# Retention and SwiGLU block on one core: keys and values of pairs five to eight loaded once, by token, one head per half of the partitions

## The chip, the cores and the metric

The kernel runs on one NeuronCore of a Trainium2 chip. The core has five engines, each with an instruction stream of its own that it works through in order: TensorE (PE in the profile, its weight loads PEld), VectorE (DVE), ScalarE (ACT), GpSimd (POOL) and SyncE (SP, which only issues transfers). ACT and POOL can issue transfers too. The metric is device time in microseconds; the time before is the median of three runs, 1016.25 us (1015.04 to 1018.67).

## The reference

Batch 8, 8 heads, 576 tokens, 64 dimensions per head, all float32; then a feed-forward block with 512 model dimensions and 1536 hidden ones on 4608 tokens.

```python
scores = scale * np.matmul(q, k.transpose(0, 1, 3, 2))
gamma = 1.0 - 2.0 ** (-5.0 - np.arange(H))
Dmat = np.where(rel >= 0, gamma[:, None, None] ** rel[None, :, :], 0.0)   # rel = query position - key position
ret = scores * Dmat[None, :, :, :]
attn_out = np.matmul(ret, v)
x = attn_out.transpose(0, 2, 1, 3).reshape(B * S, H * D)
g = x @ w_gate
silu = g * (1.0 / (1.0 + np.exp(-g)))
return silu * (x @ w_val) @ w_out
```

## The kernel before

**Attention.** A *pair* i is two heads of one batch: batch i // 4, heads 2p and 2p + 1 with p = i % 4; there are 32 pairs. A head's 576 tokens are 9 *chunks* of 64. Inside a chunk the scores are computed and masked; what earlier chunks contribute goes through a running 64x64 *state* per head (keys times values, scaled by a power of gamma). Every matmul of the attention is 64x64, in a quarter of the TensorE array: rows by the half of the partitions in which the operands lie, columns by the half in which the result comes out.

**One tick.** `tick(t)` moves three pairs on by one stage. On TensorE, in this order: `own_values(t-2)` (masked scores times values, inside chunks), `new_states(t-1)` (keys times values into `z`), `earlier_values(t-2)` (state times query), `scores(t-1)` (into `sc`). Then come *pieces* for the other engines, for ticks 4 to 9 in this order: `copies` of pair t-1 (L584: ScalarE copies half of `z` out of PSUM into `even`) and `keys` of pair t (L507: ScalarE scales the keys in place); `outputs` of pair t-2 (L629, L658: VectorE scales results into `x_odd`); the mask `own` of pair t-1 (L580: VectorE multiplies `sc` by the decay table `near` into `ret`); `last`, `pairs`, `odd`, `evens` (L590, L596, L603, L608: VectorE builds the states); and two VectorE transposes by 32x32 blocks (L492) that make `qT` and `kT` of pair t. `sc` and `z` share the two PSUM banks of the tile `inner`: columns 0 to 255 of each bank hold scores, columns 256 to 511 hold `z`. `kT` is one buffer: it can be rewritten only after `scores(t-1)` has read it.

**Loads.** For pairs 4 and up `load(i)` brings q and k in an arrangement of 32x32 blocks (L282, four transfers each) that the block transpose turns into a full transpose, and, for the "whole" pairs 4 to 19, k a second time and v once by token (L287, one transfer each, the two heads' tokens running through all 128 partitions). `chunk(i, hl, c)` says in which half of the partitions and in which columns chunk c of head hl lies: in whole pairs the half alternates with the chunk. So in `own_values` the even and the odd chunks of a whole pair are two groups, and an empty instruction on TensorE that waits for the first group stands ahead of `earlier_values` (L549).

**The weights and the first token tile.** While pairs 4 to 9 go through, TensorE computes the first 512 tokens of the feed-forward block: `up0(f)` for f = 0 to 11 (L853) writes the gate product of hidden block f into bankA and the value product into bankB for even f, bankC and bankE for odd f; ScalarE then reads the first (Silu, L856) and VectorE the second (L857). `down0` (L864) follows and uses the four banks in the order A, B, C, E. The weights come as 18 blocks of 1 MB in raw form; each half block j goes through `split(j)` (two ScalarE instructions, L389 and L390) and `rounding(j)` (two VectorE instructions, L406 and L407), two buffers deep: `split(j + 2)` overwrites what `rounding(j)` has read. The next raw block is requested from ScalarE's queue (from SP's for the first five) after a split. Blocks 24 and 28 (j) hold the weights of f = 10.

**The order.** Everything is issued in the order in which it is written (`manual_schedule`), and each engine keeps it. The list `plan` weaves the parts: tick 4 after the first rounding, ticks 5, 6, 7, 8, 9 after `up0` of f = 3, 5, 7, 10, 11. GpSimd has `end_loads` (L687, L692: 20 transfers for the last chunk of the first batch) ahead of all this, and its sums of output weights (L886) behind. Lines 701 to 726 (`end_...`) deal with that last chunk of the first batch in ticks 6 and 7.

Of the kernel before, what the change touches and what calls it, by code (L numbers as in the profile page):

```python
# [22 lines left out]
def tables(gamma, scale, L):  # L23

    g, at = np.array(gamma), np.arange(L)
    lane = np.arange(2 * L)[:, None]
    both = lambda t: np.repeat(t, L, axis=0).reshape(-1, 2 * L, t.shape[1]).transpose(1, 0, 2).reshape(2 * L, -1)
    twice = lambda t: np.concatenate([t, t])
    half = [np.repeat(g.reshape(-1, 2), L, axis=1).T ** (lane % 32 + 32 * r) for r in range(2)]
    pieces = scale * np.stack(half, axis=2).reshape(2 * L, -1)
    runs = scale * (g[None, :, None] ** ((4 * lane[:, :, None] + np.arange(4)) % L)).reshape(2 * L, -1)
    parts = [twice((g[:, None] ** -at).T), twice((g[:, None] ** (L - at)).T),
             both(g[:, None] ** L), both(g[:, None] ** (2 * L)), pieces, runs, both(scale * g[:, None] ** at),
             both((scale * g[:, None] ** at).reshape(-1, 2, L)[:, ::-1].reshape(-1, L))]  # L40
    return np.concatenate(parts, axis=1).astype(np.float32)


# [88 lines left out]
def kernel(  # L132
# [107 lines left out]

    loaded = {}

    def whole(i):

        return HP <= i < needed(2) - 2

    def scaled(i):

# [5 lines left out]
    def load(i):  # L254

        b, p = divmod(i, HP)
        t = kp.tile([P, NC * D], F32, tag="v", name="v", bufs=4)
        late = [rest[:, dn_at + 1280 * (i - 2) + 640 * n :][:, 0 : NC * D] for n in range(2)] if 1 < i < HP else None
        kn = late[1] if late else kp.tile([P, NC * D], F32, tag="kn", name="kn")
        queue = nc.sync  # L260
        if i < HP:
            qk = late[0] if late else ld.tile([P, 2, S // SQ, SQ], F32, tag="qk", name="qk").rearrange("p n j d -> p (n j d)")[:, 0 : NC * D]
            queues = (nc.sync, nc.scalar if i < 2 else nc.sync)
            heads = range(2 * p, 2 * p + 2)
            blocks = lambda a: a[:, 0:CW].rearrange("p (c h d) -> p h c d", h=2, d=D)
            for h, queue in zip(heads, queues):
                if scaled(i):
                    queue.dma_start(out=early[i][:, ts(h % 2, CW // 2)], in_=q[b, h, 0:CW].rearrange("(p c) d -> p (c d)", c=NFULL))
                else:
                    queue.dma_start(out=blocks(qk)[:, h % 2], in_=q[b, h, 0:CW].rearrange("(c p) d -> p c d", p=P))  # L270
            for h, queue in zip(heads, queues):
                queue.dma_start(out=blocks(kn)[:, h % 2], in_=k[b, h, 0:CW].rearrange("(c p) d -> p c d", p=P))
            for h in heads:
                queues[i % 2].dma_start(out=blocks(t)[:, h % 2], in_=v[b, h, 0:CW].rearrange("(c p) d -> p c d", p=P))
        else:
            if i == needed(1) - 3:
                qk = rest[:, 4096 : 4096 + 2 * S].rearrange("p (n j d) -> p n j d", n=2, d=SQ)
            else:
                qk = ld.tile([P, 2, S // SQ, SQ], F32, tag="qk", name="qk")
            for n, src in enumerate((q, k)):  # L280
                for a in range(P // SQ):
                    queue.dma_start(  # L282
                        out=qk[a * SQ : (a + 1) * SQ, n],
                        in_=src[b, 2 * p + a // 2, :, (a % 2) * SQ : (a % 2 + 1) * SQ].rearrange("(j t) d -> t j d", t=SQ))
            for dst, src in ((kn, k), (t, v)):
                if whole(i):
                    queue.dma_start(out=dst.rearrange("p (g d) -> p g d", d=D), in_=tokens(src, b, p))  # L287
                    continue
                for hl in range(2):
                    queue.dma_start(out=dst[:, 0:CW].rearrange("p (c h d) -> p c h d", h=2, d=D)[:, :, hl, :],  # L290
                                    in_=src[b, 2 * p + hl, 0:CW, :].rearrange("(c p) d -> p c d", p=P))
            if not whole(i):
                queue.dma_start(out=t[:, CW : CW + D], in_=v[b, 2 * p : 2 * p + 2, CW:S, :])
        loaded[i] = (qk, kn, t)

    def chunk(i, hl, c):

        if whole(i):
            g, r = divmod(NC * hl + c, 2)
            return half[r], slice(g * D, (g + 1) * D)  # L300
        if c + 1 == NC:
            return half[hl], slice(CW, CW + D)
        return half[c % 2], slice((2 * (c // 2) + hl) * D, (2 * (c // 2) + hl + 1) * D)
# [144 lines left out]
    def transposes(i):  # L448
# [34 lines left out]
        else:  # L483
            if light(i):
# [3 lines left out]
                    for r in range(2):  # L488
                        nc.scalar.activation(out=src[:, r], in_=src[:, r], func=AF.Copy, scale=piece[:, 2 * p + r : 2 * p + r + 1])
                pieces.append(scale_q)  # L490
            for n, t in enumerate((qT, kT)):
                pieces.append(lambda n=n, t=t: nc.vector.transpose(out=t, in_=qk[:, n].rearrange("p j d -> p (j d)")))  # L492

        every = slice(0, P)

        def keys():
            blocks = kn.rearrange("p (g d) -> p g d", d=D)
# [12 lines left out]
            return [lambda: (keys(), pieces[0]())] + pieces[1:]  # L510
        return [keys] + pieces

    straight, exchanged = [(slice(0, P), slice(0, P))], [(half[0], half[1]), (half[1], half[0])]

    def value(i, hl, c):

# [7 lines left out]
    def own_values(i, n=0):  # L524

        s, ret = st[i], places(i)[0]
        cs = [a + d for a in (1 - n, 5 - n) for d in (0, 2)] if whole(i) else range(0 if n else NC - 1)
        for c in cs:
            for hl in range(2):
                rows, at = chunk(i, hl, c)  # L530
                start = n == 0 and c in (cs[:2] if whole(i) else (0, 1))
                m = nc.tensor.matmul(value(i, hl, c), s["v"][rows, at], ret[rows, c % 2 if whole(i) else hl, c // 2],  # L532
                                     start=start, stop=start, skip_group_check=True)
        if n == 0:
            s["own"] = m
# [26 lines left out]
    def scores(i, alone):  # L562
# [6 lines left out]
        for c in range(NFULL):  # L569
            for hl in range(2):  # L570
                for r in range(2):
                    at = ts(2 * c + r, L)
                    nc.tensor.matmul(sc[chunk(i, hl, 2 * c + r)[0], r if whole(i) else hl, c], kT[half[hl], at], qT[half[hl], at],
                                     start=True, stop=True, skip_group_check=True)

    def masked(i):
        p, (ret, ret_last, state) = i % HP, places(i)

        def own():
            nc.vector.tensor_tensor(out=ret, in0=sc, in1=near[:, 2 * p : 2 * p + 2].unsqueeze(2).to_broadcast([P, 2, NFULL, L]),  # L580
                                    op=ALU.mult)

        def copies():
            (nc.vector.tensor_copy if vector(i + 1) else nc.scalar.copy)(out=even, in_=z[:, 0])  # L584

        odd_states = state[:, 1:].rearrange("p (c r) d -> p c r d", r=2)[:, :, 1]
# [96 lines left out]
    def end_loads():  # L683
# [5 lines left out]
                        in_=src[0, a // 2 : H : 2, CW + j * SQ : CW + (j + 1) * SQ, (a % 2) * SQ : (a % 2 + 1) * SQ].rearrange("n t d -> t n d"))  # L689
        for hl in range(2):  # L690
            for x in range(2):
                nc.gpsimd.dma_start(out=end_v[half[hl ^ x], 2 * x : 2 * x + 2],  # L692
                                  in_=v[0, 4 * x + hl : 4 * x + 4 : 2, CW:S].rearrange("n t d -> t n d"))

    def end_transposes():
# [9 lines left out]

    def end_masks():
        for x in range(2):
            nc.vector.tensor_tensor(out=end_ret[:, 2 * x : 2 * x + 2], in0=end_at[x], in1=near[:, 5 * x : 5 * x + 3 : 2], op=ALU.mult)

    def end_own(x):  # L710
        for n, _, hl in [e for e in ends if e[1] == x]:
            rows = half[hl ^ x]
# [24 lines left out]
    def tick(t, lo=HP, hi=NP, spread=False, then=None):  # L737
# [832 lines left out]
```

## Time and profile before

| | |
|---|---|
| median of three runs | 1016.25 us (1015.04, 1016.25, 1018.67) |
| the profiled execution | 1014.55 us, of which 1012.8 us is the span from its first to its last instruction |
| granted TensorE clock | 1.000 |
| busy in the span | PE 99%, PEld 82%, DVE 70%, ACT 28%, POOL 55% |
| mean DMA rate | 192 GB/s |
| mean busy share of the 16 DMA engines, first eight of 40 slices, tenths | 9 9 9 9 8 6 6 9 |
| transfer packets | 278892, of which 212552 are under 512 bytes |

Times in the timeline count from the start of the span. The busy shares are averages over very different stages: tick 4's transposes run at 43 us, ticks 5 to 9 begin on TensorE at 54.8, 70.0, 86.5, 110.3 and 119.6 us. In rows of instructions the first number is the start, the second the duration; what stands in brackets is the time that the engine was idle before it and what ended the wait. A group of several instructions in one row ("x3") has the time from its first start to its last end.

### The profile page before, as it was taken

How to read it: one execution, taken by the hardware profiler on the slowest of the kernel's cores; microseconds unless marked ns; L12 is line 12 of the kernel's file. 1: busy time of each engine (PE TensorE's matmuls, PEld its weight loads, DVE VectorE, ACT ScalarE, POOL GpSimd, SP SyncE). 2: the span in 40 equal slices, each digit the busy share in tenths (PEclk: the TensorE clock that was granted, in tenths of full speed). 3: DMA queues.
4: the chain of work that ended last, by engine and by line, in shares of the span. 5: the costliest groups of instructions: out<-in, count | busy, mean ns of one | idle time of the engine just before them, and what ended most of it. 6: DMA issues, size and time to landing. Idle time of an engine off the chain costs nothing.

```text
span 1012.8 us, 21319 instructions
## 1 busy us (share of the span) xinstructions
PE 1000.9 (99%) x8336; PEld 825.5 (82%) x8336; DVE 710.9 (70%) x1206; ACT 286.7 (28%) x636; POOL 561.8 (55%) x589
## 2 busy tenths in 40 slices
PE   6999999999999999999999999999999999999998
PEld 5655555888888888888888888888888888888887
DVE  4488887677875766977777678866575767566645
ACT  4565522132423312133422202233220012232110
POOL 3400359979375228575564157746672586566514
PEclk9999999999999999999999999999999999999999
DMA  9999866967587787647677777434454554445553
GB/s 245 261 288 272 192 216 234 264 193 214 138 238 207 217 231 193 198 156 196 184 202 206 198 179 217 154 133 159 161 172 141 154 189 147 148 155 180 182 159 102
DMA packets 278892, 194.38 MB, mean 192 GB/s; under 512 B 212552, under 2 KB 246088, under 8 KB 278792
## 3 DMA queue, kind: packets, MB, share of 16 engines
q1 hardware_dynamic: 251464, 94.70, 36.7%
q10 hardware_dynamic: 26688, 97.92, 29.1%
q8 instruction: 66, 1.08, 0.5%
q0 software_dynamic: 640, 0.39, 0.2%
q14 instruction: 34, 0.28, 0.1%
HBM read 154.04 MB, written 38.93 MB: 191 GB/s over the span
## 4 chain that ended last, share of the span: by engine, by line
PE 94%; DVE 2%; DMA 1%; POOL 1%; SPq 0%; issue 0%; ACT 0%; DVEq 0%; ACTq 0%; POOLq 0%
PE bankB L1186 12%; PE bankC L1186 11%; PE bankA L1186 11%; PE bankE L1186 11%; PE bankB L1392 7%; PE bankC L1392 7%; PE bankE L1392 6%; PE bankA L1392 6%; PE outer L532 2%; PE bankE L853 2%; PE bankA L853 2%; PE outer L1186 2%; PE inner L1186 2%; PE bankB L853 2%; PE outer L559 2%; PE bankC L853 2%
## 5 line engine op out<-in xcount | busy, mean ns | idle before, releaser
L1042 POOL TENSOR_TENSOR rest<-rest 128x512 f32<-128x512 f32 (+1 forms) x139 | 148.0, 1076 | 159.9 <-DVE rest L1042 112.5
L1201 POOL TENSOR_TENSOR arena<-rest,io 128x256 f32<-128x256 f32 x168 | 123.9, 750 | 89.4 <-ACT io L1200 88.9
L1200 ACT ACTIVATE io<-rest 128x256 f32<-128x256 f32 x192 | 79.3, 417 | 200.0 <-DVE rest L1042 140.0
L1186 PE MATMUL bankB<-rest,arena 128*128 128x256 f32 x448 | 114.5, 380 | 0.0
L1042 DVE TENSOR_TENSOR rest<-bankB,rest 128x512 f32<-128x512 f32 x116 | 78.5, 685 | 40.5 <-PE bankB L1186 28.5
L1186 PE MATMUL bankC<-rest,arena 128*128 128x256 f32 x416 | 106.3, 380 | 0.0
L1186 PE MATMUL bankA<-rest,arena 128*128 128x256 f32 x412 | 104.8, 379 | 0.0
L1042 DVE TENSOR_TENSOR rest<-bankA,rest 128x512 f32<-128x512 f32 x111 | 75.2, 685 | 40.8 <-PE bankA L1186 19.3
L1042 DVE TENSOR_TENSOR rest<-bankC,rest 128x512 f32<-128x512 f32 x110 | 74.5, 683 | 38.0 <-PE bankC L1186 23.4
L1042 DVE TENSOR_TENSOR rest<-bankE,rest 128x512 f32<-128x512 f32 x106 | 71.7, 684 | 36.2 <-PE bankE L1186 17.6
L1186 PE MATMUL bankE<-rest,arena 128*128 128x256 f32 x372 | 94.9, 380 | 0.3 <-DVE rest L1042 0.3
L1186 PEld LDWEIGHTS bankB<-rest,arena 128*128 128x128 f32 x448 | 84.7, 190 | 11.9 <-DVE rest L1042 0.2
L1186 PEld LDWEIGHTS bankC<-rest,arena 128*128 128x128 f32 x416 | 78.5, 190 | 11.4 <-DVE rest L1042 0.8
L1186 PEld LDWEIGHTS bankA<-rest,arena 128*128 128x128 f32 x412 | 78.1, 190 | 10.9 <-DVE rest L1042 0.2
L1186 PEld LDWEIGHTS bankE<-rest,arena 128*128 128x128 f32 x372 | 70.3, 190 | 10.4 <-DVE rest L1042 0.8
L1042 POOL TENSOR_TENSOR arena<-arena 128x256 f32<-128x256 f32 (+1 forms) x76 | 70.3, 947 | 11.1 <-PE bankC L1186 9.0
L886 POOL TENSOR_TENSOR rest<-rest 128x512 f32<-128x512 f32 x21 | 28.5, 1377 | 72.1 <-DVE rest L407 58.5
L1392 PE MATMUL bankB<-arena 128*128 128x256 f32 x264 | 61.0, 381 | 0.0
L1392 PE MATMUL bankE<-arena 128*128 128x256 f32 x264 | 60.8, 380 | 0.0
L1392 PEld LDWEIGHTS bankE<-arena 128*128 128x128 f32 x264 | 50.0, 190 | 6.9
L1392 PEld LDWEIGHTS bankB<-arena 128*128 128x128 f32 x264 | 49.8, 190 | 6.9
L1392 PE MATMUL bankC<-arena 128*128 128x256 f32 x240 | 55.2, 379 | 0.0
(270 smaller groups left out, 1876.0 us busy)
## 6 DMA issues: line engine op xcount, KB each, us to landing
arena<-up ACTq DMA_DIRECT2D x63, 896.0 KB, 4.6
arena<-dn ACTq DMA_DIRECT2D x65, 384.0 KB, 3.1
arena<-dn SPq DMA_DIRECT2D x39, 384.0 KB, 3.1
out_dram<-rest SPq DMA_DIRECT2D x31, 256.0 KB, 3.4
qk<-in_q_dram SPq DMA_DIRECT2D x108, 72.0 KB, 3.1
qk<-in_k_dram SPq DMA_DIRECT2D x108, 72.0 KB, 3.4
dn<-rest SPq DMA_DIRECT2D x26, 256.0 KB, 2.8
up<-arena SPq DMA_DIRECT2D x13, 512.0 KB, 5.6
```

The source lines that it names most:

```text
L532: m = nc.tensor.matmul(value(i, hl, c), s["v"][rows, at], ret[rows, c % 2 if whole(i) else hl, c // 2], start=start, stop=start, skip_grou ...
L559: nc.tensor.matmul(xr[half[hl]] if c + 1 == NC else value(i, hl, c), state[half[hl], c, :], s["qT"][half[hl], ts(c, L)], start=False, stop ...
L853: nc.tensor.matmul(bank, w, xs[0][:, c, :], start=(c == 0), stop=(c == HP - 1))
L886: eng.tensor_tensor(out=dst, in0=srcs[0], in1=srcs[1], op=ALU.add if op[0] == "add" else ALU.subtract)
L1042: eng.tensor_tensor(out=out, in0=a, in1=b, op=ALU.add if sign > 0 else ALU.subtract)
L1186: m = nc.tensor.matmul(b[:, g * TB : (g + 1) * TB], w[:, g], x, start=(opens and g == 0), stop=True, skip_group_check=True)
L1200: nc.scalar.activation(out=s, in_=src[:, 0:TB], func=AF.Silu)
L1201: (nc.vector if busy and o != 2 and qd + 1 < NQ else nc.gpsimd).tensor_tensor(out=hid[:, qd, 2 * H + h, 2 * T + t], in0=src[:, TB : 2 * TB ...
L1392: nc.tensor.matmul(b[:, m * TB : (m + 1) * TB], lhs[:, qd, ts(m, P)], w[:, qd], start=(opens and qd == 0 and m == 0), stop=(qd == NQ - 1), ...
```

## The change

Pairs 4 to 7 (the second batch) become "natural" pairs, and no longer count as whole. Their k and v are each loaded once, by token, with a head in each half of the partitions (two transfers each); the four transfers of k in blocks are gone. `turn_keys` makes `kT`: VectorE transposes `kn` by 32x32 blocks in one instruction, which leaves the two off-diagonal blocks of each 64x64 chunk in each other's place; GpSimd copies one of them aside (into the unused k half of the `qk` tile), and four ScalarE copies exchange them across the halves of 32 partitions. One ScalarE instruction then scales the keys with a new table column per pair (`own_key`) in place of two. `turn_keys` is issued first of a tick's pieces (ticks 4 to 7), where the transpose of k stood last and `keys` stood beside `copies`.

Since both operands of a head now lie in its own half, the results of odd chunks change halves: `new_states` writes odd chunks of `z` in the other half, ScalarE's copy brings them back in two instructions instead of one, and the mask `own` (ticks 5 to 8) becomes three VectorE instructions, one for even chunks and two that change halves for odd ones. The waiting instruction ahead of `earlier_values` is dropped for these pairs. The end pieces of the first batch are treated in the same way (`end_masks` three instructions instead of two).

```diff
+             np.repeat(g.reshape(-1, 2), L, axis=1).T ** (L - lane % L)]
...
+    def natural(i):
+        return HP <= i < 2 * HP
     def whole(i):
-        return HP <= i < needed(2) - 2
+        return 2 * HP <= i < needed(2) - 2
...
-            for n, src in enumerate((q, k)):
+            for n, src in enumerate((q,) if natural(i) else (q, k)):
...
+                if natural(i):
+                    for hl in range(2):
+                        queue.dma_start(out=dst[half[hl]].rearrange("p (c d) -> p c d", d=D),
+                                        in_=src[b, 2 * p + hl].rearrange("(c t) d -> t c d", t=L))
+                    continue
...
     def chunk(i, hl, c):
+        if natural(i):
+            return half[hl], slice(c * D, (c + 1) * D)
...
+    own_key = tab[:, NCOL + 2 * HP * L :]
...
-            for n, t in enumerate((qT, kT)):
+            for n, t in enumerate((qT,) if natural(i) else (qT, kT)):
...
+        def turn_keys():
+            kept = qk[:, 1, 0:NC]
+            at = kT.rearrange("p (c x t) -> p c x t", x=2, t=SQ)
+            nc.vector.transpose(out=kT, in_=kn)
+            nc.gpsimd.tensor_copy(out=kept, in_=at[:, :, 1])
+            for lo in (0, D):
+                one, two = slice(lo, lo + SQ), slice(lo + SQ, lo + D)
+                nc.scalar.copy(out=at[one, :, 1], in_=at[two, :, 0])
+                nc.scalar.copy(out=at[two, :, 0], in_=kept[one])
+            nc.scalar.activation(out=kn[:, 0:CW], in_=kn[:, 0:CW], func=AF.Copy, scale=own_key[:, p : p + 1])
+        if natural(i):
+            return [turn_keys] + pieces
...
-                    nc.tensor.matmul(z[half[hl], r, c], s["kn"][chunk(i, hl, 2 * c + r)], s["v"][rows, at],
+                    nc.tensor.matmul(z[half[hl ^ r if natural(i) else hl], r, c], s["kn"][chunk(i, hl, 2 * c + r)], s["v"][rows, at],
...
-        wait = nc.tensor.nop()
-        tc.add_manual_dep(wait.ins, s["own"].ins.name,
-                          mybir.DependencyInfo(mybir.DependencyClass.Sync, mybir.DependencyReason.DATA), reason="row halves")
+        if not natural(i):
+            wait = nc.tensor.nop()
+            tc.add_manual_dep(wait.ins, s["own"].ins.name,
+                              mybir.DependencyInfo(mybir.DependencyClass.Sync, mybir.DependencyReason.DATA), reason="row halves")
...
         def own():
+            if natural(i):
+                for rows, to, x in [(every, every, 0)] + [(*e, 1) for e in exchanged]:
+                    nc.vector.tensor_tensor(out=ret[to, x], in0=sc[rows, x], in1=near[rows, 2 * p + x].unsqueeze(1).to_broadcast(list(sc[rows, x].shape)),
+                                            op=ALU.mult)
+                return
...
         def copies():
+            if natural(i):
+                for rows, to in exchanged:
+                    nc.scalar.copy(out=even[to], in_=z[rows, 1])
+                return
...
-                    nc.vector.scalar_tensor_tensor(out=at, in0=even[:, c], scalar=step[:, p : p + 1], in1=z[:, 1, c],
+                    one, two = (z[:, 0, c], even[:, c]) if natural(i) else (even[:, c], z[:, 1, c])
+                    nc.vector.scalar_tensor_tensor(out=at, in0=one, scalar=step[:, p : p + 1], in1=two,
...
     def end_masks():
         for x in range(2):
-            nc.vector.tensor_tensor(out=end_ret[:, 2 * x : 2 * x + 2], in0=end_at[x], in1=near[:, 5 * x : 5 * x + 3 : 2], op=ALU.mult)
+            for rows, to in exchanged if x else straight:
+                nc.vector.tensor_tensor(out=end_ret[to, 2 * x : 2 * x + 2], in0=end_at[x][rows], in1=near[rows, 5 * x : 5 * x + 3 : 2], op=ALU.mult)
...
         outputs = to_x(t - 2)[0] if lo <= t - 2 < hi else lambda: None
+        if lo <= t < hi and natural(t):
+            pieces.append(keys)
+            keys = lambda: None
```

More of the change, by code (lines that the diff above doesn't have):

```diff
@@ L39, in tables @@
              both(g[:, None] ** L), both(g[:, None] ** (2 * L)), pieces, runs, both(scale * g[:, None] ** at),
-             both((scale * g[:, None] ** at).reshape(-1, 2, L)[:, ::-1].reshape(-1, L))]
+             both((scale * g[:, None] ** at).reshape(-1, 2, L)[:, ::-1].reshape(-1, L)),
+             np.repeat(g.reshape(-1, 2), L, axis=1).T ** (L - lane % L)]
     return np.concatenate(parts, axis=1).astype(np.float32)
@@ L291, in load @@
                                     in_=src[b, 2 * p + hl, 0:CW, :].rearrange("(c p) d -> p c d", p=P))
-            if not whole(i):
+            if not whole(i) and not natural(i):
                 queue.dma_start(out=t[:, CW : CW + D], in_=v[b, 2 * p : 2 * p + 2, CW:S, :])
@@ L511, in transposes @@
         return [keys] + pieces
-    straight, exchanged = [(slice(0, P), slice(0, P))], [(half[0], half[1]), (half[1], half[0])]
+    every = slice(0, P)
+    straight, exchanged = [(every, every)], [(half[0], half[1]), (half[1], half[0])]
     def value(i, hl, c):
@@ L527, in own_values @@
         cs = [a + d for a in (1 - n, 5 - n) for d in (0, 2)] if whole(i) else range(0 if n else NC - 1)
+        parity = whole(i) or natural(i)
         for c in cs:
@@ L531, in own_values @@
                 start = n == 0 and c in (cs[:2] if whole(i) else (0, 1))
-                m = nc.tensor.matmul(value(i, hl, c), s["v"][rows, at], ret[rows, c % 2 if whole(i) else hl, c // 2],
+                m = nc.tensor.matmul(value(i, hl, c), s["v"][rows, at], ret[rows, c % 2 if parity else hl, c // 2],
                                      start=start, stop=start, skip_group_check=True)
@@ L572, in scores @@
                     at = ts(2 * c + r, L)
-                    nc.tensor.matmul(sc[chunk(i, hl, 2 * c + r)[0], r if whole(i) else hl, c], kT[half[hl], at], qT[half[hl], at],
+                    rows = half[hl ^ r] if natural(i) else chunk(i, hl, 2 * c + r)[0]
+                    nc.tensor.matmul(sc[rows, r if whole(i) or natural(i) else hl, c], kT[half[hl], at], qT[half[hl], at],
                                      start=True, stop=True, skip_group_check=True)
@@ L691, in end_loads @@
             for x in range(2):
-                nc.gpsimd.dma_start(out=end_v[half[hl ^ x], 2 * x : 2 * x + 2],
+                nc.gpsimd.dma_start(out=end_v[half[hl], 2 * x : 2 * x + 2],
                                   in_=v[0, 4 * x + hl : 4 * x + 4 : 2, CW:S].rearrange("n t d -> t n d"))
@@ L707, in end_masks @@
         for x in range(2):
-            nc.vector.tensor_tensor(out=end_ret[:, 2 * x : 2 * x + 2], in0=end_at[x], in1=near[:, 5 * x : 5 * x + 3 : 2], op=ALU.mult)
+            for rows, to in exchanged if x else straight:
+                nc.vector.tensor_tensor(out=end_ret[to, 2 * x : 2 * x + 2], in0=end_at[x][rows], in1=near[rows, 5 * x : 5 * x + 3 : 2], op=ALU.mult)
     def end_own(x):
         for n, _, hl in [e for e in ends if e[1] == x]:
-            rows = half[hl ^ x]
+            rows = half[hl]
             m = nc.tensor.matmul(end_at[x][half[hl ^ x], n], end_v[rows, 2 * x + n], end_ret[rows, 2 * x + n],
```

## The prediction

> **What bounds the kernel now.** I read the busy time in stretches first: the start, the next 25 us, the tail, and the stretches in which the changed pairs run.
>
> ```profile
> 0.00:25.00 25.00, 17.36 (x406) 14.29 (x407) 12.54 (x29) 10.42 (x21) 9.14 (x17) 1.00 1.06 244
> 25.00:50.00 25.00, 24.82 (x197) 15.70 (x196) 11.81 (x24) 12.60 (x26) 12.51 (x23) 1.00 1.09 265
> 900.00:1012.00 112.00, 109.39 (x507) 95.95 (x505) 63.26 (x83) 20.13 (x42) 53.96 (x45) 1.00 0.49 156
> ...
> 55.00:73.00 18.00, 18.00 (x254) 9.69 (x251) 14.84 (x32) 11.68 (x22) 0.00 (x0) 1.00 1.09 298
> 90.00:113.00 23.00, 23.00 (x185) 11.19 (x184) 19.41 (x41) 14.74 (x27) 1.38 (x1) 1.00 1.04 265
> ```
>
> The columns after the length are PE, PEld, DVE, ACT and POOL, then clock, DMA share, GB/s. PE is busy 1000.9 of 1012.8 us. Of the 11.9 us left, 7.64 lie in the first 25 us, 0.18 in the next, 2.6 in the tail: some 1.5 us of waiting remain in all the rest. The start comes before the first changed transfer (28 us) and the tail is far behind the changed pairs, so waits that the change removes can give at most about 1.5 us. TensorE bounds the stage; VectorE follows at 82 to 84% there, and the transfers are saturated (share over 1) without holding TensorE up.
>
> So the question is how far VectorE and ScalarE may fall behind before TensorE feels it. The timeline around tick 7 and behind tick 8 answers:
>
> ```profile
> 89.58 0.37 ACT L584 COPY even<-inner 128x256 f32<-128x256 f32 x1 [2.38 <-PE inner L573]
> 90.52 0.69 DVE L580 TENSOR_TENSOR ret<-inner,near 128x512 f32<-128x512 f32 x1
> 95.48 0.43 DVE L406 TENSOR_SCALAR arena<-rest 128x512 int32<-128x512 int32 x1
> 95.94 0.68 ACT L389 ACTIVATE rest<-rest 128x512 f32<-128x512 f32 x1 [3.99 <-DVE arena L406]
> 100.19 0.60 ACT L856 ACTIVATE io<-bankA 128x512 f32<-128x512 f32 x1
> ...
> 103.27 1.45 PE L853 MATMUL bankA<-rest,arena 128*128 128x512 f32 x3
> ...
> 123.66 0.68 DVE L857 TENSOR_TENSOR arena<-bankE,io 128x512 f32<-128x512 f32 x1
> 124.38 0.30 PEld L864 LDWEIGHTS bankE<-rest,arena 128*128 128x128 f32 x2 [0.57 <-DVE arena L857]
> ```
>
> Read it backwards. After a tick's pieces VectorE goes on with a rounding (95.48), a ScalarE split waits for that (95.94), and splits and roundings hand over to each other until ScalarE reads bankA (100.19 to 100.79), the product of f = 8. TensorE wants bankA for f = 10 at 103.27. **First margin: 2.4 us.** Behind tick 8, VectorE's last read of bankE ends at 124.34, and the weight load of TensorE's next use of bankE had waited for it, 0.57 us against 0.24 between its neighbours. **Second margin: about 0.1 us.** VectorE's way there from tick 8's pieces (112.14) has no gap.
>
> **The change, part by part.** *Prices.* Exchange copies (32x288, four per tick): the trace has no such copy. A ScalarE scaling from SBUF to SBUF with 288 columns has 523 ns, with a number from a table; without one, 512 columns have 621 ns, and PSUM copies grow by 107 ns from 128 to 256 columns, so 288 columns are 0.43 us. Back to back such instructions overlap by about 0.1: 0.33 each; upper bound 0.43 each, from the 523 ns.
>
> ```profile
> L489 ACT ACTIVATE qk<-qk,tab 128x288 f32<-128x288 f32 x22 | 10.4, 523 | 0.0
> L917 ACT ACTIVATE rest<-rest 128x512 f32<-128x512 f32 x1 | 0.6, 621 | 0.0
> L626 ACT COPY rest<-outer 64x256 f32<-64x256 f32 x8 | 2.9, 367 | 0.1
> L1440 POOL COPY last_near<-near 128x256 f32<-128x256 f32 x1 | 0.4, 397 | 0.1
> ...
> DVE ret L580 <- ACT even L584: 13.6, 10, 2.3
> ```
>
> GpSimd's copy aside: 0.397 for 256 columns, so 0.45 for 288; upper bound 0.84, from its two-operand instruction (750 ns for 256). Key scaling: 549 ns for 320 columns grown to 512: 0.71, followed after 0.62. Copies of z: two at 0.37, the second ending 0.64 after the first starts. Masks: three 0.43 apart (as L629 x3, 1.28) against 0.6: +0.7 us of VectorE per tick. End masks +0.25.
>
> *The new chain.* The transposition of k stays one VectorE instruction (0.73) but moves ahead of the masks; behind it hang GpSimd's copy (0.04 + 0.45 + 0.04, hand-overs as between L584's end and L580's start at 29 us), four exchanges (1.32), the scaling (0.62), and only then, on ScalarE's queue, the copies of z (0.64 + 0.04): **3.15 us** from the end of the transposition. The last row above says what waits for them: VectorE's mask waits for ScalarE's copy of z ten times. Queued behind the copies on ScalarE are the next split, its weight request and the Silu; behind the mask on VectorE the states, the transpose of q and the roundings. The trace cannot tell whether each mask half waits for both copies; I let it. [...]
>
> *Tick 4* has no masks. GpSimd's queue is busy with `end_loads` until 46.5 us, so the copy aside ends at 46.95 and the rest on ScalarE at about 49, where ScalarE now waits for weights until 49.29: hidden. Those weights stand behind load(4) on SP, which loses 4.93 us of issuing (32.07 to 37.0), so they come earlier, and if GpSimd is free by 45, ScalarE is up to 1.7 us ahead (no more helps: tick 5's transposition needs `scores(4)`, over at 56.1). I take 1.0 ahead, range 0.3 to 1.7.
>
> *Tick 5.* VectorE reaches its pieces at 57.87 - 1.0 = 56.87; transposed 57.60; half masks from 60.75; `last`, two steps of 0.43 later, at 61.6 against 58.46: +3.15. The transposition (0.66) no longer comes at the end: the next rounding is 2.5 late. *Tick 6*: VectorE comes free at 71.86 + 2.5 (the read of bankE at 71.25 and 0.61 to the next instruction; its wait for TensorE until 72.61 absorbs the rest), `last` at 74.36 + 0.73 + 3.15 + 0.86 = 79.1 against 74.66: +4.4; outputs (1.45) run inside the wait. Next rounding -0.66 + 0.25: 4.0 late. *Tick 7*: free at 87.85 + 4.0 (likewise from the read at 87.24), `last` at 96.6 against 91.13: +5.45, next rounding 4.8 late.
>
> *First stall.* ScalarE's read of bankA ends at 100.79 + 4.8: 2.4 us too late for 103.27. *Second.* VectorE ends the roundings ahead of tick 8 at 109.96 + 4.8, the next read of bankB at 115.4, where TensorE (2.4 late) would have had it at 114.5: 0.9 behind, plus 0.7 of masks, less the margin of 0.1: 1.5 us. *On TensorE*: as many matmuls; the quarters now alternate without repeats and the waiting instruction is gone; 32 records take 0.47 us, and with at most a tenth of that to win per group it is -0.1 (0 to -0.3). *SP*: eight transfers instead of ten per pair; all come earlier. The wider table adds 16 bytes per partition: nothing. Later weight requests move with the splits that need them.
>
> Sum: 2.4 + 1.5 - 0.1 = **+3.8**; the span becomes 1016.6. The profiled execution had 1014.55 in all, 1.7 below the median; against the median 1016.25 the forecast is 1020.0.
>
> **Rivals.** *Absorbed* (+0.5 to +2.0, 1017.5): ScalarE gets its full 1.7 ahead at tick 4 (-0.7), halves wait singly (-0.8), the exchanges are shorter; the first stall nearly goes, the second, fed by masks, stays. For: 3.99 us of ScalarE idling at 95.94 shows that it has room. Against: its copies stand in one queue.
>
> *Not slower* (1015.5): the transfers decide. Four times 295 KB less, all in 128-byte pieces, in saturated stretches; weights arrive up to 4.9 us sooner, ScalarE works ahead of VectorE and both stalls vanish, up to 0.7 us of TensorE's remaining waits too. It decides if splits start before 45 us and tick 5 is not held by `scores(4)`. Against: only one ScalarE wait for weights over 1 us stands in the stage, at 49.29, and TensorE waits for none. [...]
>
> *Worse* (+5.2 to +7, 1022.3): the chain has the upper prices, 0.4 more on GpSimd and 0.4 on ScalarE per tick, 2.4 in three ticks, with VectorE slowed beside GpSimd (its L407 at 105.4 took 1.55 beside a GpSimd sum, else 0.69).
>
> **How the numbers follow.** Forecast (+2 to +5.2) 0.58, of which three quarters lie above +3.05, that is 0.3%, about what a measurement of this kernel can tell from no change; worse 0.17; absorbed 0.17; not slower 0.08, with 0.03 of it below -0.3% by the runs' own scatter (1015.0 to 1018.7). Slower 0.43 + 0.17 = 0.60; faster 0.03; same 0.37. Range 1016.6 (+0.4) to 1023.0 (+6.8).
>
> **What would show it.** In the changed profile: masks (L580's successor) starting over 3 us after the transposition of `kn` and right after the copies of z; a TensorE wait ahead of bankA for f = 10 by ScalarE's Silu; a wait ahead of the first bankE of `down0` by VectorE; everything later shifted. Wrong it is if roundings keep their times, if exchanges take under 0.25 us, or if stalls appear elsewhere, by a late load above all.

## The result and the profile after

The changed kernel takes **1027.72 us** (median of six runs, 1026.34 to 1029.68), the kernel before on the same chip 1017.75 us (six runs): a ratio of 1.0104 (95% interval 1.0089 to 1.012), or some 10 us slower. The forecast was 1020.0 us, at most 1023.0: the direction was right, the size was not. The profiled execution took 1027.91 us with a span of 1026.2 us, 13.4 us over the span of before; the execution of before that was profiled lay 3.2 us below the median of these six runs, so the two spans differ by more than the two medians.

TensorE's waits, in the view of waits of the changed kernel (total, times, longest), hold one new row, and its timeline says where:

```profile
PE bankA L898 <- ACT io L901: 7.8, 3, 5.0
```

```profile
75.61 5.29 PE L898 MATMUL bankA<-rest,arena 128*128 128x512 f32 x8 [2.36 <-ACT io L901]
94.78 3.70 PE L898 MATMUL bankA<-rest,arena 128*128 128x512 f32 x8 [0.48 <-ACT io L901]
113.75 6.69 PE L898 MATMUL bankA<-rest,arena 128*128 128x512 f32 x8 [4.98 <-ACT io L901]
```

These are the first products of f = 6, 8 and 10; before, they start at 72.46, 89.43 and 103.27 us without a wait, and their eight matmuls take 3.70, 3.70 and 3.60 us. So TensorE loses 7.8 us in waits and another 1.6 (5.29 - 3.70) and 3.1 us (6.69 - 3.60) in matmuls that run slowly behind two of the waits. With 0.7 us that the kernel is late already at f = 4 (56.75 against 56.03) this is 13.2 of the 13.4 us. Behind f = 11 nothing more is lost: the place of the predicted second stall has no wait.

Why the matmuls are slow, the view of stretches shows (columns as in the prediction; the third value from the right is the granted clock; a count in brackets includes instructions that only reach into the stretch):

```profile
75.00:80.00 5.00, 4.39 (x7) 2.00 (x8) 3.82 (x7) 3.39 (x6) 0.00 (x0) 0.66 1.11 287
80.00:85.00 5.00, 5.00 (x13) 2.16 (x12) 2.35 (x7) 3.98 (x9) 0.43 (x1) 1.00 0.69 206
90.00:113.00 23.00, 18.29 (x203) 9.22 (x201) 17.86 (x40) 14.93 (x27) 0.43 (x1) 1.00 0.84 207
115.00:120.00 5.00, 5.00 (x7) 1.94 (x7) 4.59 (x8) 4.66 (x9) 1.38 (x1) 0.52 1.10 335
```

From 90 to 113 us, where TensorE had been busy throughout, it is now idle for 4.7 us, and DMA is no longer saturated (share 0.84, before 1.04). From 115 to 120 us it counts as busy throughout but does half the work: 7 matmuls at a clock of 0.52, where a full clock does 13 (80 to 85 us).

ScalarE's read of bankA is late because of the chain that the prediction called the new chain. Around tick 5, and then behind tick 7, the timeline of the changed kernel reads:

```profile
60.70 0.77 DVE L512 STREAM_TRANSPOSE kT<-kn 128x576 f32<-128x576 f32 x1
61.59 0.43 POOL L513 COPY qk<-kT 128x288 f32<-128x288 f32 x1 [12.01 <-DVE kT L512]
62.05 0.43 ACT L516 COPY kT<-kT 32x288 f32<-32x288 f32 x1 [2.00 <-POOL qk L513]
63.88 0.72 ACT L518 ACTIVATE kn<-kn,tab 128x512 f32<-128x512 f32 x1
64.61 0.74 ACT L622 COPY even<-inner 64x256 f32<-64x256 f32 x2
65.39 1.30 DVE L613 TENSOR_TENSOR ret<-inner,near 128x256 f32<-128x256 f32 x3 [3.93 <-ACT even L622]
70.19 0.39 DVE L419 TENSOR_SCALAR arena<-rest 128x512 int32<-128x512 int32 x1
...
108.38 0.43 DVE L419 TENSOR_SCALAR arena<-rest 128x512 int32<-128x512 int32 x1
113.10 0.60 ACT L901 ACTIVATE io<-bankA 128x512 f32<-128x512 f32 x1
```

From the transposition to the masks each row waits for the one above it, by its data or by its place in ScalarE's queue (three further exchange copies, at 62.52, 62.97 and 63.43 us, stand between the third row and the fourth). VectorE, which should go on with the masks, stands still for 3.93 us at tick 5, and for 2.61 us at ticks 6 and 7, where the outputs run inside the wait. The first rounding after ticks 5, 6 and 7 comes at 70.19, 89.25 and 108.38 us, before at 62.59, 78.51 and 95.48: 7.6, 10.7 and 12.9 us late. The read of bankA at 113.10 us is 12.9 us behind the one at 100.19 us.

### The profile page after: what moved, and what is told of

It is laid out like the page before. It is cut to its first block, busy times and chain, and to the rows that moved or that the text cites. A ratio compares the mean times of both kernels' runs of the same rounds, so it can differ in the third digit from the quotient of the medians.

```text
span 1026.2 us, 21355 instructions
## 1 busy us (share of the span) xinstructions
PE 1006.2 (98%) x8336; PEld 827.6 (81%) x8336; DVE 717.3 (70%) x1215; ACT 294.4 (29%) x652; POOL 562.9 (55%) x593
## 4 chain that ended last, share of the span: by engine, by line
PE 87%; DMA 4%; SPq 3%; DVE 3%; ACT 2%; issue 1%; POOL 0%; ACTq 0%; DVEq 0%; POOLq 0%
PE bankB L1231 12%; PE bankC L1231 12%; PE bankA L1231 11%; PE bankE L1231 11%; PE bankB L1437 7%; PE bankE L1437 7%; PE bankC L1437 7%; PE bankA L1437 6%; DMA qk<-in_q_dram 2%; PE outer L1231 2%; PE inner L1231 2%; PE outer L561 2%; SPq L383 1%; PE outer L589 1%; PE inner L604 1%; SPq L287 1%
## 5 line engine op out<-in xcount | busy, mean ns | idle before, releaser
L1231 PE MATMUL bankB<-rest,arena 128*128 128x256 f32 x448 | 114.5, 380 | 0.0
L1231 PEld LDWEIGHTS bankA<-rest,arena 128*128 128x128 f32 x412 | 78.2, 190 | 10.7
L1231 PEld LDWEIGHTS bankE<-rest,arena 128*128 128x128 f32 x372 | 70.2, 190 | 10.4 <-DVE rest L1087 0.4
L1437 PE MATMUL bankA<-arena 128*128 128x256 f32 x228 | 52.5, 380 | 0.0
```

The lines of the kernel that those rows point to most:

```text
L1231: m = nc.tensor.matmul(b[:, g * TB : (g + 1) * TB], w[:, g], x, start=(opens and g == 0), stop=True, skip_group_check=True)
L1437: nc.tensor.matmul(b[:, m * TB : (m + 1) * TB], lhs[:, qd, ts(m, P)], w[:, qd], start=(opens and qd == 0 and m == 0), stop=(qd == NQ - 1), ...
```

## The experiments

Ten kernels were run, each timed against the kernel before on the same chip. Three theories stood at first: that the masks are held by the order on ScalarE's queue (the copies of z stand behind the exchange; the queue theory); that the loss comes in earlier, at tick 4 or with the transfers; and that the change of halves itself, three masks and two copies of z in place of one each, costs it (the halves theory). L numbers are those of the changed kernel.

**z_first: the copies of z ahead of the exchange.** On ScalarE only the order is changed.

```diff
-            pieces.append(keys)
-            keys = lambda: None
+            pieces.append(lambda copies=copies, keys=keys: (copies(), keys()))
+            copies = keys = lambda: None
```

> The changed kernel with one order altered: in ticks 5 to 7 ScalarE's copies of z are issued ahead of turn_keys instead of behind it. Queue theory (VectorE's masks wait 2.6 to 3.9 us per tick because the copies of z stand behind the exchange on ScalarE's queue): the waits ahead of the masks go, the rounding behind tick 7 is some 4 us later than in the kernel before instead of 12.9, TensorE waits for bankA at most 1.5 us, the clock halves for one window at most: 1018 to 1021 us. Tick-4 theory (the late copy aside on GpSimd at tick 4 does the damage, the later ticks only pass it on): 1025 to 1028, hardly better. Halves theory (three masks and two copies of z instead of one each do it): 1025 to 1028.

Measured: 1020.77 us, ratio 1.004 (1.002 to 1.0059). The same instructions in another order give back 6 to 7 of the 10 us. No wait at bankA is left, and the masks follow the transposition at once. What shows instead is the second stall of the prediction, with a slow pair of matmuls (1.02 us elsewhere) behind it, in the timeline of z_first:

```profile
129.38 1.86 PE L909 MATMUL bankE<-rest,arena 128*128 128x512 f32 x2 [2.09 <-DVE arena L902]
```

This execution was 2.37 us late already ahead of everything that the edit touches (the bankA products that start at 33.98 us before start at 36.35, the bankE products of f = 3 at 53.68, before at 51.31). In the view of waits TensorE's wait at L561 is 2.0 us, before 1.0; no view accounts for the rest of the 2.37 us. From there to f = 10 it lost only another 0.2 us (105.83 against 103.27).

**tick4_vector: the kept copy of tick 4 on VectorE**, so that it does not wait for GpSimd, which is issuing `end_loads`.

```diff
-            nc.gpsimd.tensor_copy(out=kept, in_=at[:, :, 1])
+            (nc.vector if i == HP else nc.gpsimd).tensor_copy(out=kept, in_=at[:, :, 1])
```

> The changed kernel, but at tick 4 alone the copy aside is made by VectorE, not by GpSimd, whose queue is issuing transfers then. Queue theory: tick 5's transposition starts some 4 us earlier, the lateness behind ticks 5, 6 and 7 falls from 7.6, 10.7 and 12.9 us to about 3, 6 and 8.5; bankA of f = 6 and 8 comes in time, the wait for bankA of f = 10 stays, 4 to 6 us with a halved clock: 1022 to 1026. Tick-4 theory: 1018 to 1020. If the transfers were late instead, ScalarE's first split after tick 4 would wait for weights until about 52 as before: 1026 to 1028.

Measured: 1027.39 us, ratio 1.0113 (1.0097 to 1.0128), as the changed kernel. The exchange of tick 4 is over at 47.3 us now, but the first split behind it starts no earlier (53.30 us, 52.06 in the changed kernel), as in the last case of the expectation, and TensorE's waits only fall elsewhere, as the timeline of tick4_vector shows:

```profile
53.30 0.67 ACT L402 ACTIVATE rest<-rest 128x512 f32<-128x512 f32 x1 [5.96 <-DMA rest<-in_moe_w_gate_dram]
76.93 3.70 PE L898 MATMUL bankA<-rest,arena 128*128 128x512 f32 x8 [2.48 <-ACT io L901]
96.06 5.40 PE L898 MATMUL bankA<-rest,arena 128*128 128x512 f32 x8 [2.00 <-ACT io L901]
115.02 3.70 PE L898 MATMUL bankA<-rest,arena 128*128 128x512 f32 x8 [3.27 <-ACT io L901]
```

Here ScalarE waits for the weight block that SP requests behind load(4). So the late copy on GpSimd alone is not what the 10 us are made of: without it the weights are what is late. The three waits say something else: behind the shortest the eight matmuls take 5.40 us, behind the other two 3.70 (as behind a fourth, of 1.22 us, at f = 4).

**halves_only: the natural layout and the change of halves, no exchange.** k is loaded a second time in blocks, and kT is transposed from these as before.

```diff
-            for n, src in enumerate((q,) if natural(i) else (q, k)):
+            for n, src in enumerate((q, k)):
...
-            for n, t in enumerate((qT,) if natural(i) else (qT, kT)):
+            for n, t in enumerate((qT, kT)):
...
-            nc.vector.transpose(out=kT, in_=kn)
-            nc.gpsimd.tensor_copy(out=kept, in_=at[:, :, 1])
-            for lo in (0, D):
...
```

> The changed kernel with the layout kept (a head per half, results of odd chunks in the other half, three masks, two copies of z) but without turn_keys: k is loaded a second time in blocks, as before, and transposed whole; the keys are scaled beside the copies of z. Queue theory: only 0.7 us of masks per tick are left, 2 to 3 us of lateness behind tick 7, about the margin of 2.4 us: 1017 to 1020. Halves theory: 1025 to 1028.

Measured: 1023.65 us, ratio 1.007 (1.0054 to 1.0087), slower than expected, for a reason of its own. With blocks and tokens both, SP reaches the weight block at 48.29 us (38.86 before), the first split after tick 4 starts at 55.57 us, and TensorE pays for it at f = 4, in the timeline of halves_only (its L889 is the changed kernel's L898):

```profile
60.19 5.40 PE L889 MATMUL bankA<-rest,arena 128*128 128x512 f32 x8 [3.90 <-ACT io L892]
```

The wait and the slow matmuls (5.40 us against 3.70) are 5.6 us of its loss. After that it gains little lateness from tick to tick: the first roundings after ticks 5, 6 and 7 are 7.2, 7.8 and 9.4 us late. The three masks and the two copies of z are thus not the main cost; but as a measure of the halves alone this run is spoilt.

**hold3 and hold1: the kernel before, TensorE held ahead of f = 10** by three tiny chained transfers, or one; nothing else is changed.

```diff
+        if f == 10:
+            plan.append(hold)
         plan.append(lambda f=f: up0(f, range(HP)))
...
+    def hold():
+        src = hid0[8][:, 0:16]
+        for m in range(3):
+            moved = nc.gpsimd.dma_start(out=relay[:, m], in_=src)
+            src = relay[:, m]
+        wait = nc.tensor.nop()
+        tc.add_manual_dep(wait.ins, moved.ins.name, ...)
```

> The kernel before, with TensorE held ahead of f = 10 by three small transfers in a row (nothing else is changed; the other engines get ahead meanwhile). It measures what a wait of TensorE costs by itself. Clock theory (after a wait of some us the granted clock is half for one or two stretches of 3.4 us): a wait of s us costs s + 1.7 to s + 3.4; the matmuls on bankA of f = 10 take 5.3 to 6.7 us instead of 3.6, the granted clock in that stretch is 0.5 to 0.7. Without it: s, 3.6 us, clock 1.0. With s of about 6 to 10 us: 1025 to 1031 against 1024 to 1028.

> The kernel before, TensorE held ahead of f=10 by one tiny chained transfer instead of three: a wait of 3 to 9 us on an otherwise unchanged kernel. Clock theory: the eight matmuls of bankA behind the wait take 5.3 to 6.8 us instead of 3.6, in stretches of half clock, and the time goes up by the wait plus 1.7 to 3.1 us. Rival (the wait costs itself alone, and the slow matmuls of the changed kernel have another cause, such as its transfers): 3.6 to 3.7 us for the eight, and the time goes up by the wait alone, or less where VectorE and ScalarE use it to get ahead.

Measured: hold3 1036.97 us, ratio 1.0204 (1.0189 to 1.0219), with a wait of 18.53 us and 5.39 us for the eight matmuls behind it. hold1 1026.19 us, ratio 1.0103 (1.0077 to 1.0128). Two rows of the timeline of hold1 (L389 and L853 are the changed kernel's L402 and L898):

```profile
51.95 0.67 ACT L389 ACTIVATE rest<-rest 128x512 f32<-128x512 f32 x1 [3.82 <-DMA rest<-in_moe_w_gate_dram]
112.78 5.23 PE L853 MATMUL bankA<-rest,arena 128*128 128x512 f32 x8 [8.75 <-issue]
```

The eight matmuls lose 1.6 us (5.23 - 3.60) and 1.8 us (5.39 - 3.60) in a kernel that has nothing of the change in it, so the slow matmuls belong to the waits (in hold1 the granted clock is 0.50 from 110 to 115 us). 8.75 + 1.6 = 10.4 us is what the medians show (1026.19 - 1016.08 = 10.1); 18.53 + 1.8 = 20.3 against 20.1 (1036.97 - 1016.86, before's median there). The waits are those of single executions, 1.5 us (hold1) and 1.1 us (hold3) above their medians, so the sums agree to about 1.5 us and not to a tenth. Within that, a wait of TensorE here goes into the time in full, with the 1.6 to 1.8 us of the slow matmuls on top. The first row matters too: up to f = 10, hold1 and hold3 are the kernel before but for one small tile more, and their first split after tick 4 starts at 51.95 and 54.37 us, where the profile of before has 49.29. The arrival of that block differs by 5 us between executions of the same instructions.

**both: z_first and tick4_vector together.**

> The changed kernel with both single edits: the z copies ahead of the exchange on ScalarE (z_first), and the kept copy of tick 4 on VectorE (tick4_vector). Transfer theory (what starts the rounding after tick 4 late is the weight block that SP requests behind load(4), not GpSimd's copy): the first split of weights after tick 4 still waits for that transfer, at 53 to 54 us, and the total stays that of z_first, 1019.0 to 1022.5 us. Rival (GpSimd's late copy costs its 2.8 us once the larger loss of the masks is gone): 1017 to 1018.5.

Measured: 1018.3 us, ratio 1.0019 (1.0004 to 1.0033), below the expected 1019.0 to 1022.5 of the transfer theory and within the rival's range. The first split waited for the weight block (until 50.58 us in the profiled run), as the transfer theory said, though not until the 53 to 54 us that it gave. The intervals of z_first and both overlap, so how much of the 2 us between them (3.9 and 2.1 us over their runs of before) is due to GpSimd's copy is open. Around tick 5 the timeline of both shows the chain laid aside:

```profile
58.69 0.74 ACT L622 COPY even<-inner 64x256 f32<-64x256 f32 x2
59.30 0.77 DVE L512 STREAM_TRANSPOSE kT<-kn 128x576 f32<-128x576 f32 x1
59.99 1.27 DVE L613 TENSOR_TENSOR ret<-inner,near 128x256 f32<-128x256 f32 x3
60.66 0.43 ACT L516 COPY kT<-kT 32x288 f32<-32x288 f32 x1 [1.23 <-POOL qk L513]
64.78 0.39 DVE L419 TENSOR_SCALAR arena<-rest 128x512 int32<-128x512 int32 x1
```

The masks start as soon as VectorE has issued the transposition, while the exchange runs beside them. From the transposition to the next rounding it is 5.5 us, against 9.5 in the changed kernel (60.70 to 70.19).

**pool_exchange: the changed kernel with its order, the four exchange copies on GpSimd.**

```diff
-                nc.scalar.copy(out=at[one, :, 1], in_=at[two, :, 0])
-                nc.scalar.copy(out=at[two, :, 0], in_=kept[one])
+                nc.gpsimd.tensor_copy(out=at[one, :, 1], in_=at[two, :, 0])
+                nc.gpsimd.tensor_copy(out=at[two, :, 0], in_=kept[one])
```

> The changed kernel with the four exchange copies of a pair on GpSimd, behind its kept copy, and the order of turn_keys otherwise as it was: the scaling of kn and, behind it, the z copies no longer wait on ScalarE for the exchange. Queue theory (the masks wait only because the z copies stand in line behind the exchange): scaling starts behind the transposition, the z copies end about 2.3 us earlier, the lateness of the first rounding after tick 7 falls from 12.9 to 5 to 7 us, TensorE's waits at bankA from 7.8 to under 3, and the total is 1018 to 1022. Rival (the exchange itself is what is late: scores and later pieces wait for kT, and GpSimd at 0.44 a copy is no faster): 1026 to 1029.

Measured: 1020.23 us, ratio 1.0047 (1.0029 to 1.0064), as the queue theory expected, with a lateness behind tick 7 just under its 5 to 7 us. The exchange is still there, it only stands in another queue. The timeline of pool_exchange:

```profile
60.43 0.72 ACT L518 ACTIVATE kn<-kn,tab 128x512 f32<-128x512 f32 x1 [1.44 <-DVE kT L512]
61.95 1.30 DVE L613 TENSOR_TENSOR ret<-inner,near 128x256 f32<-128x256 f32 x3 [1.56 <-ACT even L622]
...
105.64 5.40 PE L898 MATMUL bankA<-rest,arena 128*128 128x512 f32 x8 [2.40 <-ACT io L901]
```

The scaling starts behind the transposition (59.63, 0.77 us) instead of behind the exchange, the mask's wait falls from 3.93 to 1.56 us, and the roundings are 4.2, 5.0 and 4.8 us late. The last is 2.4 more than the margin of 2.4 us; TensorE waits 2.40 us at f = 10 and loses 1.8 more in slow matmuls (5.40 us against 3.60).

**weights_first and before_weights: load(4) behind the weight block on SP**, in the kernel of both and in the kernel before.

```diff
-        if t == 3:
+        if t == HP:
             load(HP)
```

> The kernel of 'both', and load(4) issued on SP behind the weight block of tick 4 instead of ahead of it. Transfer theory: the block's request goes from 38 to 41 us back to about 32, it lands ahead of 48, and the first split after tick 4 starts at 46 to 49 instead of 53; what z_first still lost (4 us) is then 0 to 1.5 us: 1015.5 to 1018.5. Rival (load(4) is what the ticks need, and comes some 4 us later now): kT of pair 4 is transposed at 47 to 50 instead of 44 to 45, the first split is no earlier, and the total is 1020 to 1024.

> The kernel before, with only that edit: load(4) issued on SP behind the weight block of tick 4. Transfer theory: the split that started at 49.29 us behind 4.39 us of waiting for the block starts at 45 to 46, no bankA of the up projection waits for it, and the total is 1012 to 1016. Rival (load(4), 4 to 5 us later, takes the block's place): the keys of tick 4 are scaled at 48 to 50 and the split behind them on ScalarE at 50 to 52: 1017 to 1021.

Measured: 1018.59 us, ratio 1.0033 (1.0022 to 1.0044), and 1015.56 us, ratio 0.9995 (0.9986 to 1.0005): no gain in either. The block is requested at 28.6 and 27.9 us, and ScalarE no longer waits for it, but then k of pair 4 comes late: the exchange starts at 50.13 us (44.06 in both), the split behind it at 52.57; in before_weights the keys are scaled at 48.92 us instead of 43.94 and the split starts at 49.79. The transfers of this stretch are saturated (share 1.09 from 25 to 50 us in the profile of before), and here the order of the two decided only which one is late. The two times do not tell the theories apart (1018.59 lies between the two ranges, and 1015.56 in the transfer theory's range, but 0.7 us from its runs of before); the splits do, for none starts at 46 to 49 us in the one or at 45 to 46 in the other.

**all_three: the kernel of both, the exchange of ticks 5 to 7 on GpSimd.**

```diff
-                nc.scalar.copy(out=at[one, :, 1], in_=at[two, :, 0])
+                (nc.scalar.copy if i == HP else nc.gpsimd.tensor_copy)(out=at[one, :, 1], in_=at[two, :, 0])
...
```

> The kernel of 'both', and the exchange copies of ticks 5 to 7 on GpSimd; tick 4's stay on ScalarE. Queue theory to its end (what 'both' still loses is ScalarE's 1.8 us of exchange a tick, standing ahead of the next splits): the first rounding after tick 7 is at most 1 us later than in the kernel before, TensorE waits under 0.5 us at bankA and at bankE of the down projection, total 1015.0 to 1017.3 us. Rival (what is left of 'both' is the late start of the stage and its weight block, which this doesn't touch): 1017.5 to 1019.5, as 'both'.

Measured: 1018.49 us, ratio 1.0026 (1.0013 to 1.004), as both: the rival. In its profile the first roundings are 2.5, 3.3, 4.0 and 3.5 us late after ticks 4 to 7, so hardly anything is added by the ticks. Once the masks no longer wait, ScalarE's 1.8 us of exchange per tick cost nothing that shows, and what is left of the change, 2 to 3 us, is not in that queue. No version of the change beat the kernel before.

## Why the prediction was right and wrong

**Right: the mechanism.** TensorE bounds the stage; masks wait for the copies of z, these stand behind the exchange on ScalarE, the roundings and the read of bankA go late, and TensorE waits. The rule "lateness less the margin of 2.4 us" holds: 12.9 - 2.4 = 10.5, and f = 10 starts 10.48 us late (113.75 - 103.27). (Once TensorE waits for that read this is bookkeeping; what it confirms is which wait ends last.) z_first and pool_exchange, two independent ways to take the copies of z from behind the exchange, each give back 5 to 7 us. What failed are sizes that went into the rule, in two steps, and a term that was not in the sum. By terms, of the span: first stall 10.5 us where the sum had 2.4, slow clock 3.1 where it had nothing, second stall 0 where it had 1.5, TensorE's own gain 0 where it had 0.1; together 13.6, of which the span shows 13.4.

**Failed: tick 4, "hidden", ScalarE "1.0 ahead".** The first rounding after tick 4 was 2.75 us late instead (52.74 against 49.99), 3.75 us of error that every later tick inherits. The step rested on "SP: eight transfers instead of ten per pair; all come earlier", and SP's rows of the changed kernel's timeline deny that:

```profile
32.94 1.42 SPq L296 DMA_DIRECT2D kn<-in_k_dram  x2
34.47 3.87 SPq L296 DMA_DIRECT2D v<-in_v_dram  x2
39.38 0.41 SPq L383 DMA_DIRECT2D rest<-in_moe_w_gate_dram  x1
```

The weight block is requested at 39.38 us, before at 38.86. The 4.93 us of the block loads of k are gone, but kn and v now take 1.42 and 3.87 us where one transfer each took 0.50 and 1.12, and the start of the stage is later. So SP's time of issue is not a fixed price per transfer in this saturated stretch (share 1.16 from 25 to 50 us): kn and v took 0.50 and 1.12 us a transfer before, 0.71 and 1.94 here. What sets it the runs do not show. In this execution the split then stood behind the exchange (51.43 + 0.72), whose chain began when GpSimd ended `end_loads` at 49.15 us, 2.65 us later than in the profile that I read. With that wait taken away (tick4_vector) the weight block itself was later still. 49.29 us, on which the step was built, was the earliest of all executions profiled, and the unchanged code gave up to 54.37. I took a single execution's cover for the kernel's.

**Failed: the price of the chain, "3.15 us", and of the masks.** From the end of the transposition (61.47) to the masks (65.39) it is 3.92 us. The groups of the changed kernel (busy time, mean ns of one, idle time before) have the price of a copy:

```profile
L516 ACT COPY kT<-kT 32x288 f32<-32x288 f32 x8 | 3.4, 429 | 13.2 <-POOL qk L513 13.1
```

The 0.43 us of a copy and 0.72 us of the scaling (the row at 63.88) were as worked out (0.43, 0.71). But the exchange copies follow each other every 0.46 us, with no overlap, and so do the scaling and the two copies of z (0.74 us for both, 0.64 predicted); I had taken "0.33 each" where the upper bound, 0.43, was right. Four copies and the scaling make 0.6 of the 0.8 us, the copies of z 0.1, the rest is hand-overs. Behind them, `last` follows the first mask after 1.31 us (65.39 to 66.70), not after two steps of 0.43: the prediction let the first mask run inside the wait, a term that no run shows. In ticks 5, 6 and 7 alike the first mask starts only when both copies of z have ended (in tick 5 at 64.61 + 0.74 = 65.35); what holds it the runs do not show. The end pieces and outputs add about 0.3. Together this is 1.35, 1.6 and 1.4 us more than predicted in ticks 5, 6 and 7: with tick 4's 3.75 the 8.1 us between the predicted lateness of 4.8 and the measured 12.9.

**Missing: the clock behind a wait.** The sum priced a wait at its length. Half clock (0.50) behind the waits at f = 6 and f = 10 added 1.6 and 3.1 us; hold1 shows 1.6 us in the kernel before. The first lies inside the 10.5 us, the second is on top: 10.5 + 3.1 = 13.6 at f = 11.

**The second stall, 1.5,** is not there in the changed kernel, because TensorE is late itself by then. It is real: with the first stall gone it appears with 2.09 us in z_first, 0.55 in both and 0.86 in all_three. The two stalls of the sum were not independent; the larger one uses up the other. (In the working of this term, 115.4 is the end of the read of bankB, and 114.5 is the start of tick 8's pieces, 112.14 + 2.4, not TensorE's time for bankB; the difference of 0.9 is the one that was meant.)

**TensorE, -0.1:** between the last product of f = 7 and the first of f = 8, tick 7 takes 2.97 us before (86.46 to 89.43) and 3.02 in both (86.35 to 89.37): nothing gained.

**The rivals.** "Worse" had the right signs (upper prices), but in too narrow a range, since it kept tick 4 hidden. "Not slower" fell: bytes were saved in a saturated stretch (share still 1.16 from 25 to 50 us), and no wait that the time depends on became shorter. "Absorbed" would have needed the room that ScalarE has at 95.94 us to be usable; in one queue, worked through in the order of issue, it was not. Its 0.8 us for halves that wait singly (0.64 - 0.37 us in each of three ticks) did not come either, since no mask starts before both copies of z have ended.

**Open:** what makes up the 2 to 3 us that both and all_three still lose. The three masks a tick, the second margin, and the weight block's arrival each have a part in their profiles, but the block's arrival scatters by 5 us, more than the difference, so single executions cannot divide it.

## What to carry to other kernels

When an instruction is moved ahead in a queue, price what now stands between its end and the oldest waiting consumer on each queue that it passes: here two small copies behind five that were not urgent cost more than everything else in the change, and the same instructions in another order gave most of it back. Carry lateness from stage to stage with its sign, take cover for granted only when several executions show it, and in a saturated stretch do not count saved issue time as an earlier arrival (here 4.93 us of issuing went, and the weight block was requested 0.5 us later). Where TensorE is the bound, a wait can cost more than its length (in hold1 8.75 us, and 1.6 us of slow matmuls behind them).

## What the runs showed of the hardware

The eight matmuls of a bank, which take 3.60 to 3.70 us with no wait ahead of them, took 5.40 us behind waits of TensorE of 2.00 us (tick4_vector), 2.40 (pool_exchange) and 3.90 (halves_only), 5.29 and 6.69 us behind 2.36 and 4.98 (the changed kernel), 5.23 us behind 8.75 (hold1) and 5.39 us behind 18.53 (hold3). The pair behind the 2.09 us of z_first took 1.86 us instead of 1.02. Behind waits of 1.67 us (halves_only), 2.48 and 3.27 us (tick4_vector) the eight took 3.70 us. So the length alone does not decide; what does, these runs do not show.

In the changed kernel the granted clock is 0.50 from 75.42 to 78.83 us and from 112.97 to 119.79 us, for 3.41 and 6.82 us. The part of such a stretch that lies behind the wait cost about half its length: 3.2 us (75.61 to 78.83) and 6.0 us (113.75 to 119.79) cost 1.6 and 3.1.

The exchange copies, 288 columns on 32 partitions, took 0.43 us on ScalarE, which is the prediction's estimate from instructions on 128 partitions. GpSimd's copy of 288 columns on 128 partitions took 0.43 to 0.44 us. In the kernel before, ScalarE's copies of 256 columns out of PSUM (L626) took 367 ns on 64 partitions and 378 ns on 128, so half the partitions saved 11 ns there.
